# A new step list for fused banded attention and softplus FFN, with the first blocks' biases written by TensorE

## The chip, the cores and the metric

One core of one Trainium2 chip runs the kernel. The metric is the device time of one execution in microseconds (us); the number compared is the median of several runs. Engine names are as in the profile: PE is TensorE's matmuls, PEld its weight loads, DVE is VectorE, ACT is ScalarE, POOL is GpSimd, SP is SyncE, which here only starts DMAs.

## The reference

```python
# q, k, v: 4 batches x 8 heads x 768 tokens x 64; n_global = 8, n_local = 96
scores = q @ k.T / sqrt(64)
keep   = (key < n_global) | ((0 <= query - key) & (query - key < n_local))
dist   = where(key is global and not local, n_local, abs(query - key))
scores = where(keep, scores - slope[head] * dist, -1e9)        # slope[h] = 2 ** -(h + 1)
attn   = softmax(scores) @ v
x = attn.transpose(0, 2, 1, 3).reshape(3072, 512)
h = x @ w_in                                                   # 512 -> 2048
g = maximum(h, 0) + log1p(exp(-abs(h)))                        # softplus
out = g @ w_out                                                # 2048 -> 512, float32
```

A query sees at most 96 local keys and 8 global ones, so a block of 128 queries needs its own block of keys and the one before it, with the global keys copied into the first columns of the latter.

## The kernel before

**Tiling.** The 3072 tokens are 24 blocks `n` of 128, six to a batch (`first_of(n)` is the first block of a batch, which has no block before it). Two blocks make one of 12 chunks `c` of 256 tokens for the FFN. All matmuls take bf16. A block's attention is done in two halves of four heads.

**Steps.** The whole program is a list of named steps, and each engine gets its instructions in the order in which the steps stand in it; engines wait for each other by semaphores, and within an engine nothing overtakes. The steps:

- `l n`, `lv n`: loads of q and k, and of v, of a block, float32 to bf16, started by POOL (line 97). Four buffers in turn for q and k, eight for v. `wi c`, `wo c`: a quarter of w_in (line 102) or w_out (line 108), 512 KB each in bf16. Block 0's q and k come in float32 from SP (lines 84, 85) and are cast by DVE (`cq0`, `ck0`, lines 441, 444).
- `t n` (and `tq`, `tk` for the first two blocks): q and k transposed by PE through the PSUM bank `tr` and copied by DVE (lines 203, 209, 215); `d n`: the same by two DMA transposes started by SP (lines 227, 228), from block 8 on. `gk`, `gv`: copies of the global keys and values (lines 240, 244).
- `s n.half`: scores, 8 matmuls (4 in a first block) of 64 rows and 128 columns into `s_ps` (two PSUM banks, line 253), and then the bias: one DVE addition PSUM + table into `Z` in SBUF (line 267; 265 in a first block). From block 8 (`NBT`) on one step does both halves (line 284).
- `e n.half`: exp of `Z` into `Pb` by ACT (line 289). `p n.half`: PV matmuls, of 65 columns because v carries a column of ones (line 302), reciprocal and normalisation by DVE (lines 313, 316).
- `x n`: the block's result transposed for the FFN into `XT`, by PE and a DVE copy up to block 5 (lines 331, 334), by a DMA transpose from SP after that (line 327).
- `f i`: unit `i` of the FFN's first product: chunk `i // 8`, an eighth of the 2048 columns, 8 matmuls of 256 columns into one of two `hT` banks (line 347), then exp and ln(1 + e) by ACT (lines 352, 353). Units 2j and 2j + 1 of a chunk need quarter j of w_in.
- `o i`: a quarter of the second product of 128 tokens, 4 matmuls of 512 columns into bank `o` or `o2` (line 367); after four of them a DVE copy (line 373) and the store from SP. `o i` needs quarter `i % 4` of w_out. The last ones are cut finer (line 389).
- `b`, `bb`: the bias tables, ACT multiplications of a table of distances by each head's slope (lines 181, 185). `g i`: a POOL copy that reads unit `i`'s result, so that the loads after it on POOL don't start earlier (line 404). `w k`: `k` filler matmuls of zeros, 512 columns each (line 438).

**Order.** Up to unit f27 the list is written by hand (`ORDER`). After that each step has a due time in units of f (`steady`, and the loop over `todo`), and the steps run in order of it; o i follows f i by 13.9 units (`LAG`).

Of the kernel before, what the change touches and what calls it, by code (L numbers as in the profile page):

```python
# [19 lines left out]
def kernel(  # L20
# [47 lines left out]

# [10 lines left out]
    w_in_c = [const.tile([P, KM, FW], BF16, name=f"w_in{c}") for c in range(NWC)]  # L79
# [5 lines left out]
    nc.sync.dma_start(k_f[:], k[0, :, 0:P, :].rearrange("h s d -> s h d"))  # L85
# [5 lines left out]
    warm_in = const.tile([P, DM], BF16, name="warm_in")  # L91
# [9 lines left out]
    def load_w_in(c):  # L101
        nc.gpsimd.dma_start(
            w_in_c[c][:],
            moe_w_in[:, c * FW : (c + 1) * FW].rearrange("(m p) f -> p m f", p=P),
        )
# [7 lines left out]
    def load_qk(n):  # L113
        load(n, q, q_t)
        load(n, k, k_t)
# [14 lines left out]


    ident = const.tile([P, P], BF16, name="ident")
    dist_0 = const.tile([P, P], F32, name="dist_0")
    dist_d = const.tile([P, P], F32, name="dist_d")
    dist_p = const.tile([P, P], F32, name="dist_p")
# [10 lines left out]
    make_identity(nc, ident)  # L146
    load_qk(1)
    load_v(0)
    load_v(1)
    load_qk(2)  # L150
    load_qk(3)

    def tables():
        nc.vector.tensor_scalar(
            far_a[:], rampf[:], float(NL - 1), FAR, op0=ALU.is_gt, op1=ALU.mult
        )
        nc.vector.tensor_scalar(far_b[:], rampf[:], 0.0, FAR, op0=ALU.is_lt, op1=ALU.mult)
        nc.vector.tensor_tensor(far_a[:], far_a[:], far_b[:], ALU.add)
        nc.vector.tensor_tensor(dist_d[:], far_a[:], rampf[:], ALU.add)
        nc.vector.tensor_copy(dist_0[:], dist_d[:])  # L160
        nc.vector.tensor_scalar_min(dist_0[0:NG, :], dist_0[0:NG, :], float(NL))
        nc.vector.tensor_scalar(
            far_b[:], rampf[:], -float(P - NL + 1), FAR, op0=ALU.is_gt, op1=ALU.mult
        )
        nc.vector.scalar_tensor_tensor(dist_p[:], rampf[:], float(P), far_b[:], ALU.add, ALU.add)
        nc.vector.memset(dist_p[0:NG, :], float(NL))

    tables()
    ones(2, RV)

    load_w_in(0)
    load_v(2)
    load_w_in(1)
    load_v(3)

    def head_of(half, r):
        return 4 * half + 2 * ((r // 2) % 2) + r // 4

    def bias_first(half):
        for r in range(0, 8, 2):  # L180
            nc.scalar.mul(bias0[:, half, r // 2, :], dist_0[:], -slopes[head_of(half, r)])

    def bias_rest(half):
        for r in range(8):
            nc.scalar.mul(
                biasA[:, half, r, :], (dist_p if r % 2 else dist_d)[:], -slopes[head_of(half, r)]
            )

    s_ps = ps.tile([P, 8, P], F32, name="s_ps")
    x_ps = ps.tile([P, 4, D + 1], F32, name="x_ps")  # L190


    QT, KT, Zt, Pt, xt, XT = {}, {}, {}, {}, {}, {}

# [3 lines left out]
    def qk_bank():  # L198
        return ps.tile([P, 2, NPAIR, P], BF16, tag="tr", name="tr")
# [17 lines left out]
    NDT = 8  # L217
    NDX = 6
# [27 lines left out]
    def qk(n, half, dst):  # L246

        for t in range(1 if n == first_of(n) else 2):
            for mm in range(2):
                for sub in range(2):  # L250
                    m = 2 * half + mm
                    rows = slice(64 * sub, 64 * sub + 64)
                    nc.tensor.matmul(  # L253
                        dst(4 * sub + 2 * mm + t), KT[n - t][rows, m, :], QT[n][rows, m, :]
                    )

# [12 lines left out]
    def sc(n, half):  # L269

        qk(n, half, lambda r: s_ps[:, r, :])
        if n < NBT:
            add_bias(n, half)
            return
        s_lo = ps.tile([P, 4, P], F32, tag="tr", name="s_lo")
        s_hi = ps.tile([P, 4, P], F32, tag="o2", name="s_hi")
        qk(n, 1, lambda r: (s_lo if r < 4 else s_hi)[:, r % 4, :])
        add_bias(n, 0)
        step, bias = (2, bias0) if n == first_of(n) else (1, biasA)
        w = 4 // step  # L280
        Z = new_Z(n, 1)
        for i, s_i in enumerate((s_lo, s_hi)):
            regs = slice(i * w, i * w + w)
            nc.vector.tensor_tensor(Z[:, regs, :], s_i[:, 0:4:step, :], bias[:, 1, regs, :], ALU.add)  # L284

    def ex(n, half):
        nreg = 4 if n == first_of(n) else 8
        Pb = work.tile([P, 8, P], BF16, tag="Pb", name="Pb")
        nc.scalar.activation(  # L289
            Pb[:, 0:nreg, :], Zt.pop((n, half))[:, 0:nreg, :], AF.Exp, scale=inv_sqrt  # L290
        )
        Pt[n, half] = Pb

    def pv(n, half):
        first = n == first_of(n)
        Pb = Pt.pop((n, half))
        for lh in range(4):
            mm, sub = lh // 2, lh % 2
            h = 4 * half + lh
            for t in range(1 if first else 2):  # L300
                r = 2 * sub + mm if first else 4 * sub + 2 * mm + t
                nc.tensor.matmul(  # L302
                    x_ps[:, lh, :], Pb[:, r, :], v_t[n - t][:, h, :],
                    start=(t == 0), stop=(t == 1 or first),
                )
        if half == 0:
            xt[n] = (
                work.tile([P, H, D], BF16, tag="xsf", name="xsf"),
                work.tile([P, H], F32, tag="rcp", name="rcp"),
            )  # L310
        xsf, rcp = xt[n]
        h0 = 4 * half
        nc.vector.reciprocal(  # L313
            rcp[:, h0 : h0 + 4], x_ps[:, :, D : D + 1].rearrange("p h e -> p (h e)")
        )
        nc.vector.tensor_tensor(  # L316
            xsf[:, h0 : h0 + 4, :], x_ps[:, :, 0:D],
            rcp[:, h0 : h0 + 4][:, :, None].to_broadcast([P, 4, D]), ALU.mult,
        )

    def tr_x(n):
        xsf, _ = xt.pop(n)
        if n % 2 == 0:
            XT[n // 2] = xtp.tile([P, NPAIR, CT], BF16, tag="XT", name="XT")
        dst = XT[n // 2][:, :, P * (n % 2) : P * (n % 2) + P]
        if n >= NDX:
            nc.sync.dma_start_transpose(dst, xsf[:].rearrange("p h d -> p (h d)"))
            return
        tr = ps.tile([P, 2, NPAIR, P], BF16, tag="tr", name="tr")
        for m in range(NPAIR):  # L330
            nc.tensor.transpose(  # L331
                tr[:, 0, m, :], xsf[:, 2 * m : 2 * m + 2, :].rearrange("p a b -> p (a b)"), ident[:]
            )
        nc.vector.tensor_copy(dst, tr[:, 0, :, :])


    G, O = {}, {}

    def ffn1(c, u):
        if u == 0:  # L340
            G[c] = ffn.tile([P, NFB, CT], BF16, tag="G", name="G")
        hT = ps2.tile([P, 2, CT], F32, tag="hT", name="hT")
        for j in range(2):
            fb = 2 * u + j
            wc, fo = divmod(fb * P, FW)
            for m in range(KM):
                nc.tensor.matmul(  # L347
                    hT[:, j, :], w_in_c[wc][:, m, fo : fo + P], XT[c][:, m, :],
# [6 lines left out]
    def o_bank(i):  # L355
        return ps.tile([P, DM], F32, tag="o2" if i else "o", name="o")

    def ffn2(c, u):
# [4 lines left out]
        if kq == 0:  # L363
            O[c, ns] = o_bank(ns if c == 0 or c >= NCH - 3 else 0)
        o = O[c, ns]
# [35 lines left out]
    def gate(s):  # L401
# [4 lines left out]

    LAG = 13

    ORDER = """
        w8 b0 bb1 cq0 ck0 tq0 w1 tk0 w2 s0.0 b1 tq1 bb0 tk1 w1 e0.0 s0.1 e0.1
        l4 wi2 wi3 wo0 l5 lv4 wo1 lv5 wo2 wo3
        w2 p0.0 s1.0 t2 l6 lv6 p0.1 e1.0 w1 s1.1 gk2 e1.1 w2 x0 p1.0 w2 s2.0 t3 l7 lv7 e2.0 p1.1
        w2 s2.1 e2.1 gk3 w2 x1 gv2 w3 s3.0
        f0 p2.0 f1 s3.1 e3.0 p2.1 e3.1 f2 gv3 t4 gk4 f3 p3.0 x2 s4.0 p3.1 f4 f5 s4.1 x3 f6 gk5
        f7 f8 f9 t5 e4.0 o4 f10 g9 l8 o0 s5.0 e4.1 f11 o5 f12 gv4 p4.0 s5.1 o1 e5.0 p4.1 f13 gv5
        e5.1 f14 g13 l9 x4 p5.0 o2 o3 p5.1 t6 o6 f15 s6.0 e6.0 x5 o7 s6.1 t7 e6.1 p6.0 f16 g15
        lv8 f17 s7.0 o8 e7.0 d8 p6.1 x6 f18 g17 l10 s7.1 d9 e7.1 f19 p7.0 o9 f20 g19 lv9 p7.1 x7 o10 gk8
        gv8 f21 s8.0 e8.0 gk9 f22 g21 l11 o11 e8.1 f23 p8.0 d10 s9.0 o12 o13 p8.1 x8 gk10 o14  # L420
        gv9 e9.0 e9.1 f24 p9.0 f25 p9.1 x9 f26 gv10 o15 f27
    """

    def steady(n):
# [5 lines left out]
            f"x{n}": s + 3.25,  # L430
        }

    warm_ps = ps2.tile([P, DM], F32, tag="hT", name="warm_ps")

    def warm(count):

        for _ in range(count):
            nc.tensor.matmul(warm_ps[:], warm_in[:, 0:P], warm_in[:])  # L438
# [12 lines left out]
    def tr_first_k(n):  # L451
        tr = ps.tile([P, 2, NPAIR, P], BF16, tag="o2", name="tr_k")
        tr_in(tr, 1, k_t[n])
        to_KT(n, tr, nc.vector.tensor_copy if n == 0 else nc.scalar.copy)
# [3 lines left out]
        "l": load_qk, "lv": load_v, "g": gate, "w": warm, "b": bias_first, "bb": bias_rest,  # L458
        "cq": cast_q, "ck": cast_k, "tq": tr_first_q, "tk": tr_first_k,
        "wi": load_w_in, "wo": load_w_out,  # L460
    }

# [14 lines left out]
    for n in range(RV, NB):  # L477
        for name, u in (f"l{n}", 4 * n - 23), (f"lv{n}", 4 * n - 17):
            todo[f"g{u}"] = u + 1.6
            todo[name] = u + 1.7  # L480
# [40 lines left out]
```

## Time and profile before

| | |
|---|---|
| median of 3 runs | 217.68 us (217.67 to 218.86) |
| span of the profiled execution | 215.9 us |
| what lies around the span, median less span | 1.8 us |
| first matmul of unit f0 | 18.72 us |
| first matmul of the first o (o4) | 31.68 us |
| last matmul ends, last instruction | 212.8 us, 215.9 us |

| stretch, us | what runs there | PE busy, us | ACT busy | DVE busy |
|---|---|---|---|---|
| 0 to 8 | loads, tables, first transposes | 5.43 | 6.18 | 4.92 |
| 8 to 20 | attention of blocks 0 to 3, fillers | 10.45 | 6.18 | 11.60 |
| 20 to 32 | units f1 to f9, rest of block 3 | 11.87 | 11.71 | 7.65 |
| 32 to 56 | first o, blocks 4 to 7 | 24.00 | 19.87 | 14.95 |
| 56 to 150 | steady part | 94.00 | 79.07 | 52.68 |
| 150 to 216 | rest of the FFN | 62.78 | 40.42 | 23.97 |

Durations in the groups of instructions are of one instruction; a matmul's includes its way through the array, so a row of equal matmuls advances faster than the sum of their durations. How fast it advances is read from the chain that ended last, where eight matmuls of an f take 0.87 us and four of an o 0.86 us. The granted clock is 1.00 in every stretch, but the first fillers advance by 0.43 us and the later ones by 0.21 us each, so that a slow start of the array is seen in the spacing and not in that row.

### The profile page before, as it was taken

To read this page: it belongs to the slowest core of one execution; us is meant where nothing else is said; L and a number is where in the kernel's file an instruction comes from. 1 tells how busy PE (TensorE), PEld (TensorE's weight loads), DVE (VectorE), ACT (ScalarE), POOL (GpSimd) and SP (SyncE) were. 2 spreads that over 40 slices of the span, in tenths; PEclk is the share of its full clock that TensorE was granted. 3 is DMA by queue.
4 is the path that set the end of the run, shared out by engine and by line. 5 is a ranking of instruction groups with operands and counts; after the bars stand their busy time and mean duration, and the time that the engine had idled before them with its cause. 6 is when DMAs were issued, how large, how long until landed. Compare 5 with 4: busy or idle time off the path is not lost.

```text
span 215.9 us, 5010 instructions
## 1 busy us (share of the span) xinstructions
PE 208.5 (97%) x1986; PEld 140.8 (65%) x1986; DVE 115.8 (54%) x258; ACT 163.4 (76%) x266; POOL 74.1 (34%) x117
## 2 busy tenths in 40 slices
PE   7789999999999999999999999999999999999994
PEld 2356876666768666666676666667667667666553
DVE  5798933687593464464674674364574573011121
ACT  7746999849898979768878878868978978777300
POOL 8995445524253524334334334343311000000000
PEclk9999999999999999999999999999999999999999
DMA  8999999999998999999999999999992620211112
GB/s 125 152 185 183 207 183 198 164 173 145 140 130 102 146 173 147 142 147 104 155 108 128 153 115 127 154 128 110 161 140 47 98 73 8 68 52 49 49 49 97
DMA packets 109927, 27.06 MB, mean 125 GB/s; under 512 B 102608, under 2 KB 106960, under 8 KB 109904
## 3 DMA queue, kind: packets, MB, share of 16 engines
q0 software_dynamic: 77024, 13.37, 83.2%
q1 hardware_dynamic: 32880, 13.38, 31.3%
q8 instruction: 15, 0.25, 0.5%
q14 instruction: 8, 0.07, 0.1%
HBM read 27.26 MB, written 6.29 MB: 155 GB/s over the span
## 4 chain that ended last, share of the span: by engine, by line
PE 86%; ACT 6%; DVE 4%; DMA 2%; issue 1%; SPq 0%; DVEq 0%
PE o L367 38%; PE hT L347 36%; PE x_ps L302 4%; PE s_ps L253 4%; DVE Z L267 2%; ACT G L353 2%; DMA k_f<-in_k_dram 2%; ACT Pb L289 2%; ACT e_sb L352 2%; PE o L389 2%; PE s_lo L253 1%; PE tr L203 1%; DVE Z L265 1%; DVE k_t L444 0%; PE tr L331 0%
## 5 line engine op out<-in xcount | busy, mean ns | idle before, releaser
L347 PE MATMUL hT<-XT,w_in 128*128 128x256 bf16 x768 | 98.5, 273 | 0.1
L367 PE MATMUL o<-w_out,G 128*128 128x512 bf16 x368 | 92.8, 379 | 0.0
L347 PEld LDWEIGHTS <-w_in 128*128 128x128 bf16 x768 | 74.2, 98 | 25.0 <-issue 0.3
L352 ACT ACTIVATE e_sb<-hT 128x512 f32<-128x512 f32 x96 | 56.5, 588 | 21.8 <-PE hT L347 20.8
L353 ACT ACTIVATE G<-e_sb 128x512 bf16<-128x512 f32 x96 | 60.5, 630 | 3.6
L289 ACT ACTIVATE Pb<-Z 128x1024 bf16<-128x1024 f32 (+1 forms) x48 | 46.7, 977 | 11.1 <-DVE Z L267 9.8
L367 PEld LDWEIGHTS <-G 128*128 128x128 bf16 x368 | 32.2, 98 | 26.9
L267 DVE TENSOR_TENSOR Z<-s_ps,biasA 128x1024 f32<-128x1024 f32 x26 | 31.8, 1222 | 12.3 <-PE s_ps L253 12.3
L313 DVE RECIPROCAL rcp<-x_ps 128x4 f32<-128x4 f32 x48 | 8.7, 181 | 45.7 <-PE x_ps L302 45.5
L373 DVE COPY osb<-o 128x512 f32<-128x512 f32 x23 | 15.8, 685 | 26.6 <-PE o L367 26.5
L404 POOL COPY gate_t<-G 1x1 bf16<-1x1 bf16 x32 | 5.7, 178 | 67.4 <-ACT G L353 67.4
L97 POOL DMA_DIRECT2D q_t<-in_q_dram x23 | 20.5, 892 | 10.6 <-issue 5.3
L97 POOL DMA_DIRECT2D v_t<-in_v_dram x24 | 21.3, 886 | 6.4 <-PE x_ps L302 2.4
L97 POOL DMA_DIRECT2D k_t<-in_k_dram x23 | 20.5, 891 | 4.3 <-PE s_ps L253 1.9
L316 DVE TENSOR_TENSOR xsf<-x_ps,rcp 128x256 bf16<-128x256 f32 x48 | 20.4, 424 | 1.7
L302 PE MATMUL x_ps<-v_t,Pb 128*128 128x65 bf16 x352 | 18.6, 193 | 0.1
L302 PEld LDWEIGHTS <-Pb 128*128 128x128 bf16 x352 | 16.7, 98 | 2.8 <-ACT Pb L289 0.8
L253 PEld LDWEIGHTS <-KT 64*128 64x128 bf16 x352 | 10.3, 94 | 8.4 <-issue 7.0
L253 PE MATMUL s_ps<-QT,KT 64*128 64x128 bf16 x232 | 12.1, 218 | 0.9 <-DVE Z L267 0.6
L438 PE MATMUL warm_ps<-warm_in 128*128 128x512 bf16 x26 | 8.9, 445 | 1.2 <-DVE v_t L89 1.2
L284 DVE TENSOR_TENSOR Z<-s_hi,biasA 128x512 f32<-128x512 f32 x14 | 9.5, 681 | 0.0
L284 DVE TENSOR_TENSOR Z<-s_lo,biasA 128x512 f32<-128x512 f32 x14 | 9.5, 681 | 0.0
(49 smaller groups left out, 81.7 us busy)
## 6 DMA issues: line engine op xcount, KB each, us to landing
out_dram<-osb SPq DMA_DIRECT2D x23, 256.0 KB, 3.2
v_t<-in_v_dram POOLq DMA_DIRECT2D x24, 128.0 KB, 4.6
q_t<-in_q_dram POOLq DMA_DIRECT2D x23, 128.0 KB, 4.6
k_t<-in_k_dram POOLq DMA_DIRECT2D x23, 128.0 KB, 5.1
w_in<-in_moe_w_in_dram POOLq DMA_DIRECT2D x4, 512.0 KB, 9.0
w_out<-in_moe_w_out_dram POOLq DMA_DIRECT2D x4, 512.0 KB, 13.5
XT<-xsf SPq DMA_TRANSPOSE x18, 4.2
q_f<-in_q_dram SPq DMA_DIRECT2D x1, 256.0 KB, 3.3
```

Of the source, the lines that this page charges most:

```text
L97: nc.gpsimd.dma_start(dst[n][:, :, 0:D], src[b, :, i * P : (i + 1) * P, :].rearrange("h s d -> s h d"))
L253: nc.tensor.matmul(dst(4 * sub + 2 * mm + t), KT[n - t][rows, m, :], QT[n][rows, m, :])
L267: nc.vector.tensor_tensor(Z[:], s_ps[:], biasA[:, half, :, :], ALU.add)
L284: nc.vector.tensor_tensor(Z[:, regs, :], s_i[:, 0:4:step, :], bias[:, 1, regs, :], ALU.add)
L289: nc.scalar.activation(Pb[:, 0:nreg, :], Zt.pop((n, half))[:, 0:nreg, :], AF.Exp, scale=inv_sqrt)
L302: nc.tensor.matmul(x_ps[:, lh, :], Pb[:, r, :], v_t[n - t][:, h, :], start=(t == 0), stop=(t == 1 or first),)
L316: nc.vector.tensor_tensor(xsf[:, h0 : h0 + 4, :], x_ps[:, :, 0:D], rcp[:, h0 : h0 + 4][:, :, None].to_broadcast([P, 4, D]), ALU.mult,)
L347: nc.tensor.matmul(hT[:, j, :], w_in_c[wc][:, m, fo : fo + P], XT[c][:, m, :], start=(m == 0), stop=(m == KM - 1),)
L352: nc.scalar.activation(e_sb[:], hT[:], AF.Exp)
L353: nc.scalar.activation(G[c][:, 2 * u : 2 * u + 2, :], e_sb[:], AF.Ln, bias=1.0)
L367: nc.tensor.matmul(o[:], G[c][:, 4 * kq + a, ns * P : ns * P + P], w_out_c[kq][:, a, :], start=(kq == 0 and a == 0), stop=(kq == NWC - 1 a ...
L373: nc.vector.tensor_copy(osb[:], O.pop((c, ns))[:])
```

## The change

It replaces the hand-written list up to f27 by one up to f52 (token 1900 lies in block 14, whose last steps stand near its end), and changes the steps of the start:

- For blocks 0 to 3 (`NPB`) a new step `z` puts the bias into PSUM before the scores: four matmuls of `slope_id` (identity times minus a head's slope) with the table of distances, 256 columns each, 128 in block 0. The score matmuls add onto it, and the exp reads PSUM. The second half has its own two banks, `oo`; the pool of `o` and `o2` opens in their place after block 3. The distance tables are bf16.
- The second half of the SBUF bias tables is the first half times the ratio of slopes, one instruction each.
- Fillers are 256 columns wide and are held back and written into the bank that the next step uses; a step that is due anyway drops them.
- Loads of q and k are separate steps, and are no longer held by a gate before unit 15. k of block 0 is started by ACT. The identity comes from DVE.
- The order of the weights is w_in 0, 1, 2, w_out 0, 1, w_in 3, w_out 2, 3 (named `wi0 wi2 wi4 wo0 wo1 wi6 wo2 wo3`), and units f8 to f13 of chunk 1 run before and among f4 to f7.
- q and k of blocks 6 and 7 are transposed by DMA (`d6`, `d7`), and so is the result of block 4 (`y4`; `y` is `x` by DMA). For blocks 0 and 1 the second half's PV and the transposes of the result use `hT` banks.

```diff
-    nc.sync.dma_start(k_f[:], k[0, :, 0:P, :].rearrange("h s d -> s h d"))
+    nc.scalar.dma_start(k_f[:], k[0, :, 0:P, :].rearrange("h s d -> s h d"))
...
-    make_identity(nc, ident)
-    load_qk(1)
...
+    nc.vector.tensor_scalar(ident[:], rampf[:], 0.0, 1.0, op0=ALU.is_equal, op1=ALU.mult)
...
+    for h in range(H):
+        nc.vector.tensor_scalar_mul(slope_id[:, h, :], ident[:], -slopes[h])
...
     def bias_rest(half):
+        if half:
+            nc.scalar.mul(biasA[:, 1, :, :], biasA[:, 0, :, :], HALF_RATIO)
+            return
...
+    def fill(dst):
+        for _ in range(fillers[0]):
+            nc.tensor.matmul(dst, warm_in[:, 0:P], warm_in[:, 0 : dst.shape[1]])
+        fillers[0] = 0
...
     def qk_bank():
+        if fillers[0]:
+            fill(ps.tile([P, CT], F32, tag="tr", name="tr_w")[:])
         return ps.tile([P, 2, NPAIR, P], BF16, tag="tr", name="tr")
...
-                        dst(4 * sub + 2 * mm + t), KT[n - t][rows, m, :], QT[n][rows, m, :]
+                        dst(4 * sub + 2 * mm + t), KT[n - t][rows, m, :], QT[n][rows, m, :],
+                        start=not pre,
+                        stop=not pre or (mm == 1 and (t == 1 or n == first_of(n))),
...
+    NPB = 4
+    def early(n, half):
+        return (oo if half else s_ps)[:, :, :]
+    def z(n, half):
+        buf = early(n, half)
+        fill(wide(buf))
+        for j in range(4):
+            sub, mm = divmod(j, 2)
+            h = 4 * half + 2 * mm + sub
+            if n == first_of(n):
+                nc.tensor.matmul(
+                    buf[:, 2 * j, :], slope_id[:, h, :], dist_0[:], start=j % 2 == 0, stop=False
+                )
+            else:
+                nc.tensor.matmul(
+                    buf[:, 2 * j : 2 * j + 2, :], slope_id[:, h, :], dist_dp[:],
+                    start=j % 2 == 0, stop=False,
+                )
...
     def sc(n, half):
+        if n < NPB:
+            fillers[0] = 0
+            buf = early(n, half)
+            qk(n, half, lambda r: buf[:, r, :], pre=True)
+            return
...
-        nc.scalar.activation(
-            Pb[:, 0:nreg, :], Zt.pop((n, half))[:, 0:nreg, :], AF.Exp, scale=inv_sqrt
-        )
+        if n < NPB:
+            src = early(n, half)[:, 0 : 8 : 8 // nreg, :]
+        else:
+            src = Zt.pop((n, half))[:, 0:nreg, :]
+        nc.scalar.activation(Pb[:, 0:nreg, :], src, AF.Exp, scale=inv_sqrt)
...
+        w16 b0 z0.0 lq1 lk1 lk2 cq0 ck0 b1 tq0 w1 tk0 bb0 lv0 lq2 w1 z0.1 s0.0 lk3 t1 s0.1 e0.0 lq3 lv1 z1.0
+        e0.1 s1.0 z1.1 p0.0 t2 e1.0 p0.1 lv2 s1.1 gk2 z2.0 t3 e1.1 wi0 lv3 wi2 w1 bb1 lk4 w1 s2.0 p1.0 p1.1
+        lq4 lk5 lq5 e2.0 gv2 z2.1 w1 s2.1 wi4 x0 gk3 z3.0 e2.1 w1 lq6 p2.0 x1 s3.0 gk13 e3.0 z3.1 p2.1 s3.1
+        gk4 e3.1 f0 wo0 gv3 p3.0 x2 f1 lk6 lv4 wo1 w1 wi6 lv5 p3.1 f2 x3 f3 t4 f8 wo2 f9 lq7 s4.0 lk7 f10
+        lv6 f11 e4.0 s4.1 t5 wo3 lk8 gk5 f4 gv4 lq8 f12 e4.1 s5.0 e5.0 lk9 o0 d6 o4 p4.0 s5.1 lq9 f5 f13
+        p4.1 e5.1 w1 o5 y4 s6.0 o1 gv5 lv7 s6.1 f6 p5.0 f7 lk10 f14 p5.1 f15 d7 e6.0 lq10 x5 o2 f16 d8 f17
+        p6.0 o6 f18 f19 e6.1 o3 f20 s7.0 lv8 w1 o7 e7.0 o8 p6.1 lq11 s7.1 o9 o10 e7.1 lv9 d9 lq12 p7.0 gk8
+        f21 lk11 y6 o11 p7.1 f22 d10 lq13 lv10 s8.0 gk9 o12 y7 e8.0 o13 e8.1 gv8 o14 o15 f23 s9.0 lq14 o16
+        lk12 p8.0 o17 f24 g15 gk10 f25 o18 p8.1 y8 o19 e9.0 f26 e9.1 lv11 d11 f27 gv9 p9.0 o20 s10.0 p9.1
+        f28 gv10 e10.0 g13 y9 lv12 f29 e10.1 d12 o21 gk11 g9 g21 lq15 lk13 f30 p10.0 s11.0 f31 o22 e11.0
+        p10.1 o23 f32 d13 lk14 f33 e11.1 d14 lk15 o24 gv11 p11.0 s12.0 e12.0 lq16 o25 o26 lv13 lk16 g23 f34
+        y10 p11.1 e12.1 f35 g19 o27 p12.0 f36 lv14 lq17 gk12 g31 gv12 s13.0 gk14 f37 o28 lq18 e13.0 g17
+        p12.1 e13.1 f38 o29 g33 o30 f39 y11 s14.0 f40 f41 gv13 g27 p13.0 y12 f42 g25 d15 lk17 o31 f43 e14.0
+        p13.1 f44 o32 lv15 g43 gv14 o33 e14.1 gk15 lk18 f45 g29 g45 f46 p14.0 s15.0 o34 g41 lv16 y13 o35 f47
+        d16 p14.1 f48 o36 g35 e15.0 d17 gv15 g37 f49 o37 f50 g39 y14 g47 e15.1 p15.0 g49 o38 f51 f52
...
-        tr = ps.tile([P, 2, NPAIR, P], BF16, tag="o2", name="tr_k")
+        tr = qk_bank()
         tr_in(tr, 1, k_t[n])
-        to_KT(n, tr, nc.vector.tensor_copy if n == 0 else nc.scalar.copy)
+        to_KT(n, tr, nc.vector.tensor_copy)
```

## The prediction

> **What bounds the kernel now.** I read the waits first, then the timeline of the start, then the chain that ended last, then the DMA issues one by one.
>
> ```profile
> engine line waited for: us in total, times, longest us
> DVE rcp L313 <- PE x_ps L302: 45.5, 32, 2.4
> ACT Pb L289 <- DVE Z L267: 9.8, 16, 1.3
> ```
>
> DVE's own long wait costs nothing where DVE is idle anyway. The second is the one to place: ACT waits for the bias additions. The timeline puts it in the start (start, duration, engine, line; in brackets the idle time before):
>
> ```profile
> 8.69 0.63 ACT L289 ACTIVATE Pb<-Z 128x512 bf16<-128x512 f32 x1
> ...
> 11.52 1.06 ACT L289 ACTIVATE Pb<-Z 128x1024 bf16<-128x1024 f32 x1 [1.29 <-DVE Z L267]
> 13.87 1.06 ACT L289 ACTIVATE Pb<-Z 128x1024 bf16<-128x1024 f32 x1 [1.28 <-DVE Z L267]
> 15.95 1.06 ACT L289 ACTIVATE Pb<-Z 128x1024 bf16<-128x1024 f32 x1 [1.03 <-DVE Z L267]
> 18.29 1.06 ACT L289 ACTIVATE Pb<-Z 128x1024 bf16<-128x1024 f32 x1 [1.28 <-DVE Z L267]
> ```
>
> Scores, addition, exp follow each other through one pair of banks: between the first exp and f0's exp at 19.79 ACT idles 5.6 us. From there it works without a pause, and PE waits for it. At 30.36 the chain of waits passes to PE for good:
>
> ```profile
> 29.20 0.63 ACT G L353
> 29.83 0.49 ACT e_sb L352
> 30.36 1.03 PE hT L347 x8
> 31.84 0.86 PE o L367 x4
> ...
> 87.37 0.97 PE o L367 x4
> ...
> 135.46 0.97 PE o L367 x4
> ```
>
> From 87.37 to 135.46 PE does one batch, six blocks, in 48.09 us: 24 f and 24 o at 0.87 and 0.86 (41.5), so 1.1 us of attention a block. All 24 blocks at that pace are 192.4 us; the last matmul ends at 212.8. So 20.4 us are lost, and at 31.68, when the first o starts, 10 f (8.7) and 4.3 blocks (4.7) are done: 18.3 of the 20.4 go before it. What is left after that is PE's own work. **The change can win only in how early PE gets full work, and by taking work off PE.**
>
> DMA sets a second limit at the start. The landings of the weights, from single issues (last column: us from issue):
>
> ```profile
> w_in<-in_moe_w_in_dram POOLq DMA_DIRECT2D x1, 512.0 KB, 6.2
> w_out<-in_moe_w_out_dram POOLq DMA_DIRECT2D x1, 512.0 KB, 14.4
> w_out<-in_moe_w_out_dram POOLq DMA_DIRECT2D x1, 512.0 KB, 13.5
> ```
>
> Issued at 8.67, 15.2 and 26.42 they land at 14.9 (w_in 0), 29.6 (w_out 0) and 39.9 (w_out 3). POOL's loads land in the order of issue, one after the other: about 0.87 us for a block of q, k or v, 2.45 for a weight quarter.
>
> **First exp.** DVE now ends its tables at 3.79 and casts q at 4.07, k (landed at 1.26 + 4.37 = 5.63 in the chain) from 5.66 to 6.36. Added are the identity and eight slope_id multiplications, for which no row is of their type; the nearest, the 128x128 float32 comparisons, are 0.21 to 0.23 busy and start 0.15 apart: 1.3 to 2.0 us. The 0.46 copy to dist_0 halves at best. So the casts of q and k end near 5.6 and 6.35 (to 7.0). k_f, issued 0.5 earlier, lands near 5.1 and is covered. Transposes of q and k now share bank `tr`, so k's wait for QT's copy (0.41): k transposed at 6.85, KT at 7.8 (7.27 now), scores to 8.15. The exp follows directly instead of after a 0.69 addition: 8.25 against 8.69, a gain of 0.4 (−0.3 to 0.6).
>
> **Exps of blocks 0 to 3.** The eight additions (2×0.69 + 6×1.22 = 8.7 us of DVE) leave the loop. An exp of 1024 out of PSUM has no row; one of 512 has (0.588, line 352), and line 289 grows by 0.43 for the second 512 (1.048 against 0.619): 1.02. I take 1.04 and 0.6. With the second bias table, now between e1.1 and e2.0 (one ACT instruction of 128x1024, 1.05), ACT has 1.2 + 6.2 + 1.05 = 8.5 us. Where it still waits: PE. A `z` is four matmuls of 256 columns at 0.109 (line 347's pace), 0.43, and can run as soon as the exp before it has left the bank; scores 0.33, PV 0.24, q and k transposes 0.46. Between the end of s1.0 (near 10) and s1.1 stand z1.1, p0.0, t2, p0.1: 1.4 us, so e1.1 waits 0.5; e0.1, e1.0 and e3.0 wait 0.3 to 0.4 likewise. That is 1.5; with eight handings-over between engines (0.12 from scores to addition now) I take 2.1 us of idle time, for 5.6. ACT has e0 to e3 behind it at 8.25 + 8.5 + 2.1 = 18.8 (18.2 to 19.6). Before, at 24.09, it had these and two pairs of f (2×1.15): 21.8. **Gain 3.0.** Hidden: q and k of block 2 and 3 land by 9.4 and 11.1 (five and seven issues of 0.87 from 1.07, POOL without the two identity operations), w_in 0 at 15.3 behind nine loads.
>
> **To the first o.** Ten f precede it both times, and f0 now starts at 17.6. They follow s3.1, whose exp starts at 17.75. ACT: f12's bank is free when f11's exp ends, 18.8 + 7×1.15 + 0.6 = 27.5; with f12 and s5.0 28.7. PE: 17.6 + 8.7 + transposes t4, t5, x2, x3 (1.4) + scores 1.0 + PV 0.5 = 29.2. w_out 0 lands at 15.3 + three quarters (w_in 1, w_in 2, itself: 7.35) + six blocks (5.2) = 27.9, or 28.6 with a DMA transpose in between: hidden. So o0 at about 29.3 for 31.68, 2.4 earlier, with s5.0 ahead as well: 0.3.
>
> **PE work taken off.** t6, t7 (0.46 each) and x4 (0.23) go to DMA: 1.1. The rest of the list keeps the same f, o, scores and PV. Fillers are gone from the path: 26 of 512 columns become 20 of 256, all in the start.
>
> **What it costs.** (1) w_in 3 is loaded after w_out 1: by the same row of landings 34.6 instead of 26.1, and f6 wants it near 35.8 (29.3 and, between, four o, two f, PV and scores); w_out 3 lands at 43.0 for 39.9, o3 wants it near 45.4. d6, y4, d7 and d8 now run on the same DMA engines meanwhile, seven transposes; a transpose has no row alone, but from 165 to 200 us five stores and three transposes took 16.8% of 35 us, so 0.7 each: up to 5 us of delay, of which 2 to 3 reach o3 and s8.0. Both ends: 0 and 2.7; I take 0.5, because the early items have the least traffic beside them. In the Trainium skill, "DMA: Bandwidth & Descriptors", section "Queues, rings and completion order", a DMA engine takes the queues that have work in turn, packet by packet. By that rule the transposes don't wait behind POOL's backlog but stretch it, which is the upper end and would make 216.9 of the forecast; the landings of 3.9 and 4.5 us of QT and KT beside a DMA 9 tenths busy agree. (2) From f24 to f38 the list has 15 f and ten exps for 11 o: ACT 15×1.15 + 9.6 = 26.9, PE 13.0 + 9.5 + 4.8 = 27.3. ACT is as long as PE there, with two `hT` banks of slack: 0 to 1.5 of waits, I take 0.3. (3) Bank, table and POOL waits of blocks 0 to 3 are in the walk above. The first stores stand behind `d8` on SP, and only the third DVE copy (o11, near 52) would wait for them; d8 goes out near 47.
>
> Sum: 2.4 + 0.3 + 1.1 − 0.8 = 3.0. The profiled span of 215.9 becomes 212.9; with the 1.8 around it 217.7 (the median, 217.68) becomes 214.7. About 1% (2.2 us) can be told from no change.
>
> **Rivals.**
>
> *The array goes back to its slow pace (slower).* Before, the first eight fillers advance by 0.43 us, all after 4.6 by half of that. Between 6.9 and f0 the new order gives PE 19,200 columns (paired scores counted half): 8.2 us at 0.425 ns a column, 16.0 at the first pace. Fast, PE is two thirds busy there; slow, it is the bound, f0 comes 4 us later and the first f run slow too (1.5): 214.7 + 5.5 = 220.2. It decides from about 3 us lost, some 5 slow us. For it: after the first 16 fillers only two small ones stand before block 1, where 26 wide ones stood throughout. Against: the longest PE gap before, 1.14 us, did no harm, and no planned gap is much longer. The Trainium skill, "TensorE: Matmul & The Clock Gate", Part 1, puts it thus: a free-running window of about 3.4 us, fast after a busy one, slow after an idle one. By this rule gaps of 1 us are safe, but 16 fillers of 0.213 last 3.4 us, no longer than a window, as eight of 0.427 did. Chance 0.11.
>
> *The list stalls later (slower).* One block's QT or XT by DMA late in each of several blocks, a landing of 4.5 us where the list leaves 4 to 5 units of f instead of 8: from 3 us in all the gain is gone, and three such waits of 2 us make 220.7. Chance 0.07.
>
> *The waits of the start only move (no change).* w_in 3, w_out 3 and block 8 arrive late by the upper end and ACT waits by its own: 214.7 + 2.2 + 1.2 = 218.1, or half of it, 216.4. Chance 0.23.
>
> *More than that (faster).* z and transposes fit under the exps, ACT idles 0.5 us instead of 2.1, nothing waits for DMA: 214.7 − 1.6 − 0.8 = 212.3. Chance 0.17.
>
> **The numbers.** Forecast, 213.3 to 215.5: 0.42. With the last rival, faster by over 1%: 0.59; within 1%, 0.23; slower 0.18. Likeliest 214.7. The range, 211.4 to 218.9, leaves out the slow cases and the ends of the fast one.
>
> **What would show it.** e0.0 near 8.3; exps of blocks 0 to 3 without DVE as releaser, the last ending near 18.8; o0 near 29.3; f20 and o10 done near 52 instead of 56.4; from there the same pace. Wrong if fillers or transposes advance slowly after 5 us, if PE waits for w_in, w_out or KT between 33 and 56, or if ACT is PE's releaser between 60 and 95.

## The result and the profile after

| | before | after |
|---|---|---|
| median, us | 218.27 (4 runs, 217.67 to 218.93) | 227.42 (4 runs, 227.03 to 227.67) |
| span of the profiled execution, us | 215.9 | 225.3 |
| last exp of blocks 0 to 3 ends | 24.09, behind two pairs of f | 18.34 |
| first matmul of f0, of the first o | 18.72, 31.68 | 17.99, 30.80 |
| w_in 0, w_out 0, w_in 3, w_out 3 land | 14.9, 29.6, 26.1, 39.9 | 17.9, 30.7, 39.7, 49.4 |
| f20 and o10 done | 56.4 | 60.0 |

The change makes the kernel slower: ratio 1.0422, 95% interval 1.0387 to 1.0458. All ratios here are against the kernel before on the same chip and leave out runs that took over 1.5% longer than the fastest of the same kernel (two of the four of `t6_by_pe` and of `new_tail`, one of the four of three others); medians are of all runs.

The exps of the start do what they were laid for. The timeline of ACT in the changed kernel (start, duration, engine, line; idle before in brackets) no longer names DVE:

```profile
7.67 0.60 ACT L348 ACTIVATE Pb<-s_ps 128x512 bf16<-128x512 f32 x1 [1.61 <-PE s_ps L277]
...
11.19 1.02 ACT L348 ACTIVATE Pb<-oo 128x1024 bf16<-128x1024 f32 x1 [0.70 <-PE oo L277]
...
17.32 1.02 ACT L348 ACTIVATE Pb<-oo 128x1024 bf16<-128x1024 f32 x1
19.08 0.60 ACT L421 ACTIVATE e_sb<-hT 128x512 f32<-128x512 f32 x1 [0.74 <-PE hT L416]
```

Then the list of waits (total, times, longest) shows what was not there before, transposes by DMA ahead of TensorE:

```profile
PE s_ps L277 <- DMA KT<-k_t: 4.2, 1, 4.2
PE hT L416 <- DMA XT<-xsf: 2.3, 2, 1.3
PE x_ps L363 <- DVE xsf L377: 1.6, 1, 1.6
PE hT L416 <- DMA w_in<-in_moe_w_in_dram: 1.2, 2, 0.8
```

(DVE's xsf in the third had itself waited 3.7 us until a DMA transpose had read its buffer.) The first of them in the timeline of PE:

```profile
35.62 0.81 PE L438 MATMUL o<-w_out,G 128*128 128x512 bf16 x3 [0.23 <-DMA w_out<-in_moe_w_out_dram]
40.58 0.39 PE L277 MATMUL s_ps<-QT,KT 64*128 64x128 bf16 x4 [4.16 <-DMA KT<-k_t]
40.90 1.89 PE L438 MATMUL o<-w_out,G 128*128 128x512 bf16 x4
42.73 0.39 PE L277 MATMUL s_ps<-QT,KT 64*128 64x128 bf16 x4
43.05 1.89 PE L416 MATMUL hT<-XT,w_in 128*128 128x256 bf16 x8
```

s6.0 waits 4.16 us for KT of block 6, and then an o and an f take 1.89 us each, where they take about 1.03 elsewhere. The chain that ended last names what came before: k of block 6 lands at 31.57, its transpose takes 9.0 us; the XT of y7 and y9 come late in the same way.

```profile
21.87 9.68 DMA k_t<-in_k_dram
31.57 8.97 DMA KT<-k_t
...
66.30 5.82 DMA XT<-xsf
...
82.32 5.62 DMA XT<-xsf
```

The table by stretches (length; busy us and instructions of PE, PEld, DVE, ACT, POOL; granted clock; DMA; GB/s) gives the price:

```profile
32.00:40.00 8.00, 4.19 (x47) 2.87 (x45) 2.64 (x6) 5.86 (x9) 2.66 (x5) 0.92 1.94 152
40.00:45.00 5.00, 4.42 (x25) 2.16 (x26) 1.58 (x3) 0.02 (x1) 2.54 (x3) 0.50 1.76 170
...
56.00:100.00 44.00, 40.58 (x403) 27.02 (x409) 25.27 (x54) 32.19 (x49) 17.89 (x30) 1.00 1.63 153
100.00:150.00 50.00, 48.40 (x463) 34.51 (x470) 25.59 (x58) 41.25 (x65) 14.05 (x30) 1.00 1.07 116
```

PE idles 3.8 us in the first row; in the second it is busy 4.42 us, but at half the clock, so that these are worth 2.2; in the last two it idles 3.4 and 1.6. Before, PE was busy throughout from 32 to 150 us.

### The profile page after: what moved, and what is told of

Its sections match the earlier page's. It is cut to its first block, busy times and chain, and to the rows that moved or that the text cites. A ratio compares the mean times of both kernels' runs of the same rounds, so it can differ in the third digit from the quotient of the medians.

```text
span 225.3 us, 4974 instructions
## 1 busy us (share of the span) xinstructions
PE 207.8 (92%) x1964; PEld 143.7 (64%) x1992; DVE 106.9 (47%) x255; ACT 161.6 (72%) x255; POOL 73.8 (33%) x115
## 4 chain that ended last, share of the span: by engine, by line
PE 67%; DMA 21%; POOL 4%; issue 3%; DVE 2%; SPq 1%; DVEq 0%; POOLq 0%
PE o L438 30%; PE hT L416 29%; DMA XT<-xsf 8%; DMA w_in<-in_moe_w_in_dram 4%; DMA k_t<-in_k_dram 4%; DMA KT<-k_t 4%; PE x_ps L363 3%; PE s_ps L277 2%; PE o L460 2%; POOL v_t L99 1%; POOL k_t L99 1%; POOL q_t L99 1%; DVE Z L339 1%; PE s_lo L277 1%; DVE xsf L377 1%
## 5 line engine op out<-in xcount | busy, mean ns | idle before, releaser
L416 PEld LDWEIGHTS <-w_in 128*128 128x128 bf16 x768 | 73.9, 98 | 26.1 <-issue 3.3
L438 PE MATMUL o<-w_out,G 128*128 128x512 bf16 x340 | 88.1, 382 | 2.0 <-issue 0.5
L421 ACT ACTIVATE e_sb<-hT 128x512 f32<-128x512 f32 x96 | 56.4, 587 | 32.1 <-PE hT L416 32.0
L438 PEld LDWEIGHTS <-G 128*128 128x128 bf16 x368 | 33.2, 98 | 29.4 <-issue 1.1
L348 ACT ACTIVATE Pb<-Z 128x1024 bf16<-128x1024 f32 (+1 forms) x40 | 39.1, 982 | 7.8 <-DVE Z L316 7.5
L316 DVE TENSOR_TENSOR Z<-s_ps,biasA 128x1024 f32<-128x1024 f32 x20 | 24.4, 1222 | 9.3 <-PE s_ps L277 6.2
L377 DVE TENSOR_TENSOR xsf<-x_ps,rcp 128x256 bf16<-128x256 f32 x46 | 19.5, 424 | 5.5 <-DMA XT<-xsf 3.7
L277 PE MATMUL s_ps<-QT,KT 64*128 64x128 bf16 x204 | 10.9, 222 | 4.4 <-DMA KT<-k_t 4.2
L339 DVE TENSOR_TENSOR Z<-o,biasA 128x512 f32<-128x512 f32 x14 | 9.5, 679 | 0.0
L268 DVE COPY v_t<-v_t 8x512 bf16<-8x512 bf16 x16 | 6.8, 427 | 0.0
```

What stands on the lines that cost most here:

```text
L277: nc.tensor.matmul(dst(4 * sub + 2 * mm + t), KT[n - t][rows, m, :], QT[n][rows, m, :], start=not pre, stop=not pre or (mm == 1 and (t == ...
L316: nc.vector.tensor_tensor(Z[:], s_ps[:], biasA[:, half, :, :], ALU.add)
L348: nc.scalar.activation(Pb[:, 0:nreg, :], src, AF.Exp, scale=inv_sqrt)
L377: nc.vector.tensor_tensor(xsf[:, h0 : h0 + 4, :], x_b[:, :, 0:D], rcp[:, h0 : h0 + 4][:, :, None].to_broadcast([P, 4, D]), ALU.mult,)
L416: nc.tensor.matmul(hT[:, j, :], w[:, m, fo : fo + P], XT[c][:, m, :], start=(m == 0), stop=(m == KM - 1),)
L421: nc.scalar.activation(e_sb[:], hT[:], AF.Exp)
```

## The experiments

My theory after the trace: the transposes by DMA that the new list puts beside POOL's queued loads (d6, d7 and y4, by TensorE before, and d8, d9, y6, y7) land late (6.7 to 9.0 us for d6, y4, d7 and d8 in the changed kernel's trace, 4.4 to 5.8 for d9, y6 and y7), and the waits for them, with the low clock behind a wait, are most of the loss. Rivals: the loads and weights in their new order, the new start, or the list behind 60 us.

### Block 6 back to TensorE: `t6_by_pe`

```diff
-lk9 o0 d6 o4 ... o5 y4 s6.0
+lk9 o0 o4 ... o5 y4 t6 s6.0
```

> The changed kernel with block 6's q and k transposed by TensorE again (a step t6 just before s6.0) and not by the two DMA transposes of d6. Theory: K's DMA transpose (9.0 us to landing in the changed kernel's trace) is what holds TensorE for 4.2 us at 36.4, and the idle array then runs at half pace for some 5 us, which costs about 2.7 us more; without it s6.0 starts near 36.7, w_in's last quarter becomes the next wait (f6, near 38 to 39), and the median falls by 4 to 6 us from 227.4, to 221.5 to 223.5. Rival, the weights are late anyway: f6 waits for w_in until 39.7 as before, the gap only moves by one o, and the median falls by 1 us or less.

Median 228.35, ratio 1.0389 (1.0299 to 1.0478): no gain that the intervals could tell. The trace is of its slowest run, 229.96. Its waits:

```profile
PE s_ps L277 <- DMA KT<-k_t: 4.5, 3, 3.6
```

s6.0 ran at 38.84, but the 3.6 us now stand before s7.0, where KT of block 7 took 9.4 us, and the clock falls there. The number is the rival's; the mechanism is the theory's, one block later. To undo one transpose of a series tells little.

### Only d6 and d7, in the kernel before: `before_d6_d7`

```diff
-e4.0 o4 f10 ... s5.1 o1 e5.0 ... t6 o6 f15 s6.0 ... t7 e6.1
+e4.0 o4 d6 f10 ... s5.1 o1 d7 e5.0 ... o6 f15 s6.0 ... e6.1
```

> The kernel before with blocks 6 and 7 transposed by DMA instead of TensorE, issued as early as its SP queue allows. Theory, DMA transposes are slow while POOL has loads queued up: q's and k's of block 6, issued when they land (41 to 42 us), take 6.5 to 9 us instead of the 3.9 and 4.5 of later blocks; s6.0 (45.6 before) then waits 2 to 4 us, and the median is 1 to 4 us higher (219 to 222). Rival, 4.5 us as everywhere: s6.0 waits under 1 us, TensorE is rid of 16 transposes (0.9 us), and the median is 217 to 218.

226.05, ratio 1.0321 (1.0244 to 1.0398). This one part, alone, costs 7.0 us (5.3 to 8.7) on top of 218.3, more than the 1 to 4 of the theory. Timeline of PE:

```profile
43.85 1.04 PE L347 MATMUL hT<-XT,w_in 128*128 128x256 bf16 x8
50.83 0.40 PE L253 MATMUL s_ps<-QT,KT 64*128 64x128 bf16 x4 [5.94 <-DMA KT<-k_t]
```

and the landing of the KT of block 6 (issued at 42.93; last column us to landing):

```profile
KT<-k_t SPq DMA_TRANSPOSE x1, 7.9
```

The granted clock is 0.64 from 48 to 56 us. The d8 of this same run, issued when the queue of loads was empty, took 4.1 and 3.2 us.

### The same with fewer loads beside it: `d6_d7_loads_held`

```diff
-f10 g9 l8 ... f14 g13 l9 ... f16 g15 lv8 ... f18 g17 l10 ... f20 g19 lv9
+f10 ... f14 ... f16 g15 l8 lv8 ... f18 g17 l9 ... f20 g19 l10 lv9
```

> before_d6_d7 (226.05; KT6 issued at 42.93, landed 7.9 us later at 50.83, TensorE waited 5.94 us for it) with the loads of q and k of blocks 8 and 9, which were under way beside it (landed 46.98 to 52.28), held back behind the gates of f15 and f17, and those of block 10 behind that of f19. Theory (the packets of loads under way stretch a transpose): beside the transposes only what lands by about 46 is left, KT6 takes 5 to 6 us and KT7 3 to 5 (7.4 there), the wait before s6.0 is 2.5 to 4 us, and the time is 1.5 to 3.5 us lower, 222.5 to 224.5. Rival (a transpose waits for the other transposes of its queue, four in a row, and not for the loads): KT6 and KT7 take 7 us or more as before, and the time stays at 225.5 to 227.

223.66, ratio 1.0230 (1.0189 to 1.0271), 2.4 us less than before_d6_d7 in the medians, 2.0 in the ratios, whose intervals still overlap a little. The landings are clearer. The same four transposes, with the same spacing on SP; here KT of block 6 and of block 7 (7.9 and 7.4 above):

```profile
KT<-k_t SPq DMA_TRANSPOSE x1, 4.1
...
KT<-k_t SPq DMA_TRANSPOSE x1, 2.4
```

```profile
47.16 0.29 PE L253 MATMUL s_ps<-QT,KT 64*128 64x128 bf16 x4 [1.81 <-DMA KT<-k_t]
64.41 0.40 PE L253 MATMUL s_ps<-QT,KT 64*128 64x128 bf16 x8 [2.32 <-DMA KT<-k_t]
```

The wait falls from 5.94 to 1.81 (the second, 2.32, comes from holding l9, which makes block 9's k late). It is the loads under way that stretch a transpose. Other transposes beside it do not by themselves: from 118.5 us of no_early_dma_2 (below) five stand in a row on SP, 1.3 us apart and overlapping, with hardly a load under way, and each lands in 2.4 us. The Trainium skill, "DMA: Bandwidth & Descriptors", section "Queues, rings and completion order", has each DMA engine take the queues that have work in turn, packet by packet; the landings of 7.9 and 4.1 us agree.

### The low clock behind the wait: `fill_gap`

```diff
-w1 o5 y4 s6.0 o1
+w1 o5 y4 w36 s6.0 o1
```

> The changed kernel with 36 fillers of 256 columns put before s6.0, where TensorE waits 4.2 us for the DMA transpose; they add no wait of their own as long as they end by 40.6. Theory, the wait itself makes the array slow afterwards: granted clock 1.00 in 40 to 46 us, o and f there at 0.86 and 0.87 us instead of 1.82, median lower by 2 to 3 us (224.5 to 225.5). Rival, the slow clock after 40 us has another cause (power, or the free-running window alone): same clock 0.50 there and no gain beyond 0.5 us.

226.24, ratio 1.0356 (1.0307 to 1.0406), about 1.4 us less than the changed kernel, with intervals that overlap. The stretches of this run, to set against 0.92 and 0.50:

```profile
32.00:40.00 8.00, 7.77 (x76) 5.86 (x76) 3.48 (x6) 6.70 (x10) 3.39 (x4) 1.00 1.72 159
40.00:45.00 5.00, 4.73 (x49) 3.30 (x48) 2.19 (x5) 0.90 (x2) 1.90 (x3) 1.00 1.87 162
```

With the wait filled the clock stays at 1.00: idle time of the array, not the DMA, lowers it. The gain is under the 2 to 3 expected, and the trace shows two things that go against it: PE idles 4.1 us from 56 to 100 here (39.89 of 44), 0.7 more than without the fillers, and the array is slow in its start (four matmuls of 256 columns take 0.85 us at 9.63, 0.61 from 10.75 on), so that f0 starts at 18.83 for 17.99.

### All of the early transposes back: `no_early_dma_transposes`, `no_early_dma_2`

```diff
-o0 d6 o4 ... y4 s6.0 ... f15 d7 e6.0 ... f16 d8 f17 ... o3 f20 s7.0 ... d9 lq12 ... y6 o11 f22 ... y7 e8.0
+o0 o4 ... x4 t6 s6.0 ... f15 e6.0 ... f16 f17 ... o3 t7 f20 s7.0 ... t8 lq12 ... x6 o11 f22 t9 ... x7 e8.0
```

> The changed kernel with blocks 6 to 9 of q and k and the x of blocks 4, 6 and 7 transposed by TensorE again (t6, t7, t8, t9, x4, x6, x7 for d6 to d9, y4, y6, y7); loads, start and the rest of the list as they are. Theory (DMA transposes beside the queue of loads are late): no wait of TensorE for QT, KT or XT between 30 and 66 us, no half pace there, w_out3 lands before 48.5 instead of 49.36, f20 and o10 are done by 56 instead of 61. TensorE gets 4 x 0.55 + 3 x 0.28 = 3.0 us more work than in the changed kernel, and the waits for XT after 66 us (1.28, 1.06, 1.64) stay, so 220.5 to 223. Rival (the weights land late by the order of the loads itself, transposes or not): TensorE waits for w_in3, w_out2 or w_out3 as long as it did for KT, and the time stays at 225 to 228.

229.73, ratio 1.0519 (1.0483 to 1.0554). Up to 100 us it went as the theory has it: no wait of 1 us or more for a transpose, clock 1.00, w_out 3 at 45.9, o10 done at 56.1. But d8 and d9 were no longer in the list, so the order by due times issued them once more behind it, for nothing, and an XT queued behind them on SP: 5.50 us of waiting at 134.84. The second kernel leaves those out.

> no_early_dma_transposes issued the DMA transposes of blocks 8 and 9 as well, by their due times behind the list, where block 9's stood on SP ahead of an XT: TensorE waited 5.50 us for that XT before f56 at 134.84 and ran at the low clock after it. This kernel leaves those four transposes out; all else is the same. Theory (transposes by DMA beside the queue of loads are the first loss of the change): the waits before 100 us stay as they were there (0.9 for a KT, 0.9 for xsf), the one at 134.84 is gone with about 2 us of low clock, and 229.73 - 5.5 - 2 gives 222, 220.5 to 223.5, so 4 to 7 us below the changed kernel, with 3.0 us more work on TensorE. Rival (the list behind 66 us falls into waits of its own however early it starts): some other wait of 3 us or more takes its place and the time stays over 225.

223.14, ratio 1.0229 (1.0195 to 1.0264), inside the theory's 220.5 to 223.5: 4.3 us below the changed kernel with, by the estimate above, 3.0 us more work on PE. So these transposes by DMA cost about 7.3 us; d6 and d7 alone cost as much in the kernel before (7.0, with 0.9 less work on PE). Its stretches:

```profile
40.00:48.00 8.00, 7.95 (x84) 6.49 (x83) 2.53 (x8) 7.31 (x13) 4.37 (x5) 1.00 2.05 171
48.00:56.00 8.00, 7.71 (x70) 4.79 (x69) 4.91 (x8) 5.50 (x10) 1.75 (x2) 1.00 1.43 146
...
80.00:100.00 20.00, 16.16 (x169) 11.26 (x171) 9.22 (x21) 14.16 (x23) 9.83 (x17) 0.98 1.74 153
```

The rest of the list still has waits in the last row, 2.9 us for xsf and 0.7 for an XT, close to what the rival named. But this trace is of a run of 226.04; the other four took 222.8 to 223.4.

### The list behind 60 us: `old_tail`, `new_tail`, `seamed`

`old_tail` is no_early_dma_transposes up to e7.1 and the kernel before's list from gv8 on:

```diff
-e7.1 lv9 t8 lq12 p7.0 gk8 f21 lk11 x6 ...
+e7.1 lv9 x6 t8 g9 g13 p7.0 p7.1 x7 g15 g17 g19 gk8 gv8 f21 s8.0 e8.0 t9 gk9 f22 g21 lk11 ...
```

> The kernel of no_early_dma_transposes up to e7.1, from there on the list, the gates and the order by due times of the kernel before. Theory (the second part of the loss is the new list after 60 us, which places y7, y9 and y10 behind other transposes and leaves too little time to them): the waits for XT at f24, f28 and at p10 are gone, 3 to 4 us less than no_early_dma_transposes, 217 to 219.5. Rival (those waits follow from anything that is late in the start, whichever list comes behind it): within 1 us of no_early_dma_transposes.

234.42, ratio 1.0720 (1.0686 to 1.0755). It tells nothing of the list: at the seam I set the steps of block 7 one behind the other, and PE idles 3.4 us from 56 to 64; then PE waits 7.35 us for a KT at 85.56, and d8 and d9 were issued twice here too. `new_tail` has another head, that of new_start_old_list below, and takes the changed list from p7.0 on.

> The kernel of new_start_old_list (219.48) with the new list from p7.0 on, so only the list after about 60 us is the changed one. Theory: the waits for XT at f24, f28 and xsf before p10 are there without anything late ahead of them, and the time is 222 to 224. Rival (they come from the lateness before 60 us): 219 to 220.5, with no wait of TensorE over 1 us for XT.

222.67 in the median (220.24 to 224.12), ratio 1.0112 (1.0065 to 1.0159) against 1.0051 of its base: 1.3 us for the list, not 3 to 4, but from two runs. The trace, of the run of 220.24, has no wait for an XT over 0.4 us, as the rival says: there the late XTs of the changed kernel follow from what was late ahead of them. Whether the runs near 224 have such waits is not known.

`seamed` has the changed start and order of loads, the transposes of the kernel before, its list from f24 on, and the steps between laid apart:

```diff
-o0 d6 o4 ... o5 y4 s6.0 o1 gv5 lv7 s6.1 f6 p5.0 ... f15 d7 e6.0 ... o3 f20 s7.0 ... d9 lq12 p7.0 gk8
+o0 o4 ... o5 x4 o1 t6 gv5 lv7 f6 s6.0 p5.0 s6.1 ... f15 e6.0 ... t7 o3 f20 s7.0 ... d9 lq12 p7.0 o11 f21 lk11 p7.1 y7 gk8 ...
```

> The changed start and order of loads and weights, blocks 6 and 7 and x4 transposed by TensorE as in the kernel before (x4 and t6 with an o or f between them), d8, d9, y6, y7 by DMA as there, and from f24 on the list, the gates and the due times of the kernel before; the steps from p7.0 to f23 are laid so that no two steps of one block follow each other. Theory (the start is worth about 1 to 2 us, and all of the loss is in the early DMA transposes and in the list behind them): no wait of TensorE of 1 us or more behind 32 us, granted clock 1.00 there, f20 and o10 done by 56, and 216 to 218.5 us against 218.3 for the kernel before. Rival (the order of loads with w_in3 and w_out3 late is a loss by itself, or the seam is): 219 to 223, with waits for w_in, w_out or G between 33 and 60 us.

220.37, ratio 1.0106 (1.0054 to 1.0158): the rival's time. Its waits:

```profile
PE hT L416 <- DMA w_in<-in_moe_w_in_dram: 1.6, 2, 1.1
PE s_ps L277 <- DMA KT<-k_t: 1.1, 1, 1.1
...
PE o L438 <- DMA w_out<-in_moe_w_out_dram: 0.8, 1, 0.8
```

They don't stand where the rival had them, between 33 and 60 us: w_in is waited for between 17 and 22, w_out at 31.60, and the KT, of a transpose by DMA that the kernel before has too, at 63.60. So the new start with its order of loads, and the seam, which this run does not tell apart from it, are no gain but about 2.3 us of loss. The next three take the start with the old order of weights.

### The start alone: `new_start_old_list`, `early_v`, `early_v_f8`

`new_start_old_list` has the new steps of blocks 0 to 3 and, from f0 on, the list, loads and gates of the kernel before.

```diff
-... lk2 ... lv0 lq2 ... lk3 ... lq3 lv1 ... lv2 ... wi0 lv3 wi2 ...
+... lv0 ... lq2 lk2 ... lq3 ... lk3 lv1 ... wi0 ... lv2 wi2 lv3 ... wi4 wi6 wo0 ...
```

> The changed kernel's start (biases put into PSUM for blocks 0 to 3) up to e3.1, and from f0 on the list of before with its loads, gates, order of weights, d from block 8 and DMA transposes of the result from block 6. Theory, the start is a gain and the new list loses it: f0's matmuls near 17.5 with w_in's first quarter at 15.5 to 16.5, no wait over 1 us after 32, median 214.5 to 216 against 218 before. Rival, the gain of the start is held up by the weights' landings, which stay where they were (first o at w_out's first quarter, 29.6): median 217 to 218.3.

219.48, ratio 1.0051 (1.0025 to 1.0076), above both ranges. It waited for v:

```profile
PE x_ps L363 <- DMA v_t<-in_v_dram: 3.4, 2, 1.9
```

with the clock at 0.62 and 0.53 from 18 to 22 us. `early_v` loads v1 and v2 sooner:

```diff
-s0.0 lq3 t1 s0.1 e0.0 lk3 lv1 z1.0 ... wi0 s1.1 ... lv2 wi2 lv3
+s0.0 lv1 t1 s0.1 e0.0 lq3 lk3 z1.0 ... lv2 s1.1 ... wi0 lv3 wi2
```

> new_start_old_list (219.48, where TensorE waited 1.56 us for v1 and 1.85 us for v2 and ran at 0.94 and 0.92 of the clock between 8 and 32 us) with the loads of v1 and v2 ahead of q3 and k3 and of w_in0. The start with biases in PSUM, then the list, the loads' gates and the transposes of the kernel before. Theory (the start can gain what it was laid for if its loads come in the order in which it needs them): no wait for v over 0.5 us, clock 0.98 or more from 8 us on, f0 1.5 to 2.5 us earlier than 21.66, and 216.5 to 218.2, a little below the kernel before (218.3). Rival (the weights' landing bounds the start: w_in0 and all behind it land 0.9 to 1.5 us later, so the array waits for w_in and w_out in place of v): 218.5 to 220.

218.95, ratio 1.0036 (1.0014 to 1.0058): the rival's time, and w_in 0 lands 1.3 us later, as it has it. The waits for v are gone, f0 starts at 17.92 for 21.66, 3.7 us earlier, and only 0.5 us is left of it in the time. Timeline of PE:

```profile
17.92 1.05 PE L416 MATMUL hT<-XT,w_in 128*128 128x256 bf16 x8 [0.21 <-DMA w_in<-in_moe_w_in_dram]
...
21.31 1.05 PE L416 MATMUL hT<-XT,w_in 128*128 128x256 bf16 x8 [0.55 <-DMA w_in<-in_moe_w_in_dram]
...
25.54 1.92 PE L416 MATMUL hT<-XT,w_in 128*128 128x256 bf16 x16 [0.57 <-DMA w_in<-in_moe_w_in_dram]
...
28.10 3.91 PE L416 MATMUL hT<-XT,w_in 128*128 128x256 bf16 x32 [0.31 <-DMA w_in<-in_moe_w_in_dram]
```

Each quarter of w_in is waited for as it lands, and the first o starts at 32.55, later than before. `early_v_f8` draws units ahead that need only w_in 0:

```diff
-f2 t4 gk4 f3 s4.0 x3 f4 f5 s4.1 f6 gk5 f7 f8 f9 t5
+f2 x3 f3 t4 gk4 f8 s4.0 f4 f5 s4.1 f9 f6 gk5 f7 t5
```

> early_v (218.95, where TensorE waited 0.21, 0.55, 0.57 and 0.31 us for the four parts of w_in, and 0.41 for k4, between 17.7 and 28.1 us) with f8 and f9, which need only w_in0 and x2, x3, drawn ahead of f4 and f6, and x3 ahead of t4. Theory (the waits for weights in the start can be filled with FFN units of the second chunk): the waits for w_in2, w_in3 and k4, 1.3 us together, fall to 0.3 or less, and 217.4 to 218.4. Rival (the start is short of weights as a whole, so what is done earlier there is waited for at w_out0 to w_out3, which land at 30.58 to 42.04): new waits of 0.5 us or more for w_out between 30 and 43 us, and 218.6 to 219.3.

218.84, ratio 1.0027 (1.0004 to 1.0049): the rival's time. In the trace the waits for w_in fall from 1.6 to 0.4 us, and q and k of block 5, next in POOL's queue, are waited for instead:

```profile
32.11 0.40 PE L229 MATMUL tr<-ident,q_t 128*128 128x128 bf16 x4 [0.92 <-DMA q_t<-in_q_dram]
32.94 0.40 PE L229 MATMUL tr<-ident,k_t 128*128 128x128 bf16 x4 [0.43 <-DMA k_t<-in_k_dram]
```

But this trace does not show that drawing the units ahead did it, because its array is slow in the start, which the row of the granted clock (1.00) does not tell but the spacing does. Four matmuls of a `z`, first in early_v, then here:

```profile
8.74 0.61 PE L301 MATMUL s_ps<-dist_dp,slope_id 128*128 128x256 bf16 x4
...
9.95 1.03 PE L301 MATMUL s_ps<-dist_dp,slope_id 128*128 128x256 bf16 x4
```

So f0 starts at 19.49 for 17.92, after w_in 0 has landed (18.0), and what follows is later too. What the medians show is that early_v_f8 is no faster than early_v. No version here beats the kernel before; this one comes nearest.

**The sum.** Changed kernel less no_early_dma_2, with the 3.0 us of extra work that it does: 4.3 us, which are 7.3 for the transposes by DMA less the work that they take off PE. From no_early_dma_2 to seamed, 2.8 us, of which t8, t9, x6 and x7 are 1.7 of PE work (estimated as above) and 1.1 the list. From seamed to before, 2.3 for the start, its order of loads and the seam. By the intervals of the ratios each of these differences is uncertain by 1 to 1.4 us, and the third holds a KT by DMA (1.1) as well.

## Why the prediction was wrong

**Cost (1) is the step that failed.** It booked 0.5 us for the seven transposes, "because the early items have the least traffic beside them", inside bounds of 0 to 2.7. The early items have the most: all of POOL's loads are queued there, and the row that I priced a transpose by, 0.7 us of DMA time from 165 to 200 us, is from a stretch where DMA is almost idle. The kernel before had shown more: its transposes issued at 69.44 and 70.83 us, beside loads and other transposes, took 6.8 and 6.9 us, over the medians of 3.9 and 4.5 that I went by. The bounds held only the delay that the transposes give to the loads. That delay came (w_out 3 at 45.9 without them, 49.4 with them, 3.5 of the "up to 5 us"), but PE, held by KT in this trace, waited neither for w_in 3 nor for w_out 3. They did not hold the delay that the loads give to the transposes: 9.0 us for KT of block 6 where the list leaves it under 5. Nor did they hold that a gap in PE is paid twice, as a wait of 4.16 us and as 5 us at half clock. The rule of the Trainium skill that I cited points the right way, and I took it as an upper end for the loads alone.

**The start: right up to f0, wrong in what it is worth.** e0.0 at 7.67 (forecast 8.25), the last exp done at 18.34 (18.8), an exp of 1024 out of PSUM took 1.02 (taken as 1.04), f0 at 17.99 (17.6), though f0 had waited 0.78 for w_in 0. But o0 came at 30.80, not 29.3, and w_out 0, forecast for 27.9 and so hidden, landed at 30.7. w_in 0 was issued 1.15 us later than before (9.82 for 8.67) and took 8.1 us for 6.2; every later landing stood on my 15.3 for it. It is issued later because nine loads stand ahead of it for eight before (an issue is about 0.9 us) and two of the first issues take 1.1 to 1.2 us; why the transfer takes longer is not settled. early_v shows that even with none of the other changes the gain of 2.7 is not there: the start is bound by landings as soon as DVE no longer binds it.

**PE work taken off.** The 1.1 us is real; d6 and d7, which make 0.9 of it, cost eight times that in before_d6_d7.

**Cost (2).** ACT is PE's releaser nowhere between 60 and 95; what stalls PE there are XTs by DMA.

**Rivals.** The list that stalls later had the right mechanism, given 0.07 and 220.7. Its price was too low because it stood as two-microsecond waits in the later list, without the early d6 and without the clock. The array's slow pace came too, in the changed kernel's trace not in the start, where no gap is over 1.2 us, but behind the waits. With the same steps of the start it did come there in other traces: in early_v_f8 and fill_gap as told above, and in new_tail, whose granted clock is 0.50 from 8 to 10 us behind gaps of 0.45, 0.80 and 0.19. So "gaps of 1 us are safe" does not hold: short ones can add up.

## What to carry to other kernels

Price a DMA transpose where it runs, beside whatever queues are full then, and give it the landing of the worst stretch: here 2.4 us on an idle DMA and up to 9.4 beside queued loads. Before counting an earlier start as gain, lay the landings of the next loads beside it; if they land as they are needed already, the gain is theirs to take. And add to every wait of the array of about 2 us or more a stretch at half speed, here 3.4 to 6.8 us long, or fill the gap.

## What the runs showed of the hardware

- A transpose of a 128x512 block by DMA landed 2.4 us after its issue at best. Over all traces here it took 2.4 to 4.7 us with no load of POOL under way, 2.4 to 7.8 with up to four at its issue (half of them 3.6 to 5.0), and 6.7 to 9.4 with seven or eight.
- When the granted clock falls, it falls to 0.50 for 3.4 us or twice that: added up from rows of 2 us, 3.4 in new_start_old_list, new_tail, d6_d7_loads_held and no_early_dma_2, 6.8 in the changed kernel, t6_by_pe and before_d6_d7. The low stretch begins inside a long gap (from 38.8 us in the changed kernel, whose gap is from 36.42 to 40.58) or just behind a shorter one (from 18.5 in new_start_old_list, whose gap of 1.85 ends at 18.31).
- What decides seems to be PE's idle time in a window of this length, not the length of one gap. I cut the nine traces that have a low stretch into windows of 3.41 us, counted from the edge of that stretch. At full clock, PE idled over 2 us in seven of them (2.06 to 3.41), and each was followed by a low one; of eight with 1.5 to 1.95 us three were; of those with less, none. Gaps of 1.06 to 1.64 us in the changed kernel and one of 1.81 in d6_d7_loads_held left the clock at 1.00. The Trainium skill, "TensorE: Matmul & The Clock Gate", Part 1, warns of gaps over about 3.4 us; by these runs a gap of 1.85 can be enough, so that length is not a safe limit here.
